# Casts of v for steps 4 to 7 on ScalarE, new engine orders, and other stores in two transfers, in a retention + SoLU kernel

## The chip, the core and the metric

The kernel runs on one core of a Trainium2 chip. A core has five engines, each with its own in-order list of instructions: TensorE (PE, matmuls and transposes, with its weight loads shown as PEld), VectorE (DVE), ScalarE (ACT), GpSimd (POOL) and SyncE (SP, which here does nothing but issue transfers). Engines wait for one another through semaphores. Data comes from HBM into SBUF by DMA; matmuls write PSUM. The metric is the device time of one execution in microseconds (us), the median over runs.

## The reference, cut to what matters

Inputs are q, k, v of shape 8 x 8 x 576 x 64 (batch, heads, positions, head dimension) and the weights of one feed-forward block, all float32.

```
scores = q @ k.T / 8                          # per batch and head, 576 x 576
ret    = scores * D                           # D[i,j] = gamma_h ** (i-j) for i >= j, else 0
x      = (ret @ v), heads side by side        # 4608 tokens x 512
h      = x @ w_in                             # 4608 x 1024
solu   = h * softmax(h)
ln     = (solu - mean) / sqrt(var + 1e-6) * g_ln
out    = ln @ w_out                           # 4608 x 512, float32
```

The kernel computes the first part as retention with a running state: positions are taken in windows of 256, and what lies before a window enters through a 64 x 64 state for each head instead of through scores.

## The kernel before

**Steps and tiles.** There are 18 windows: for each batch two of 256 positions (`wi` 0 and 1), and for every four batches one window that holds their last 64 positions (`wi` 2). A window is worked on in two *steps*, one for each half of the heads, so there are 36 steps `i` (two for each window), and it gives two *tiles* of 128 tokens, so there are 36 tiles `t`. Steps 4 and 5 are window 2 and give tiles 4 and 5.

**Operations of a step** (the name is that of the order lists, `x` stands for the number):

- `ldq`, `ldk`, `ldv` on SP (L363): one transfer of 256 KB each into one of five raw buffers (four of 64 KB in a `wi` 2 step).
- `sq`, `sk` (L379): scale by powers of gamma and cast to f16; `cv` (L387): cast v to f16. They run on POOL unless the table `ON` (L35) says otherwise.
- `K` on PE (L514): the new part of the state. `st` on DVE (L536) adds it, `sm` (L550) and `sc` (L554) on POOL decay it and cast it.
- `T` on PE (L403): transposes of q and k; `Te` or, joined with a transpose of a later stage, `TL` on ACT brings the result to SBUF (L441).
- `S` on PE (L489): scores; `mask` on DVE (L526) multiplies them by D. `I` on PE (L465): state part of the output; `V` (L504): the rest, added in the same PSUM tile `xy`; `xe` on ACT (L563) takes it to SBUF.

**Operations of a tile:** `M1` on PE (L571, eight 128 x 512 matmuls), `ex` on ACT (exponential, L582), `so` on DVE (L587), statistics as `bnA`, `bnB` on DVE or, for tiles 0 to 3, `va` on ACT, `fx` on ACT, `rs` on POOL; `L` on PE (transpose, L424), `Le` or `TL` on ACT, `M2` on PE (L643), `oe` on ACT (L654) and `out` on SP (L663), a store of 256 KB. There is one PSUM buffer for `h` (the result of `M1`, kept until `so`), one for `xy`, one for `s` (scores and, in turn, the result of most `M2`).

**Weights.** `lwi` and `lwo` load w_in and w_out in four transfers of 512 KB each; `wi` casts w_in, `wg` scales w_out by g, `WM` on PE (L706) forms column means and `wc` on DVE (L717) subtracts them. `M1_0` needs all `wi`, `M2_0` all `wc`.

**What sets the order.** `plan` (L123) lists all operations with their engine, dependences and buffers. Each engine issues its operations in the order of a key. `FIRST` (L42) and `LAST` (L78) spell the beginning and end out by hand; between them the key grows by 4.92 for each step. `order_ops` (L224) only models when each would start; from it the program takes the interleaving in which the instructions are emitted, and how many matmuls on zeros (L836) to put into expected gaps on PE before `M2_0`. They keep TensorE busy and change no result. On each engine the list is followed strictly: an operation that waits holds back all behind it on that engine.

Of the kernel before, what the change touches and what calls it, by code (L numbers as in the profile page):

```python
# [31 lines left out]
OFF = 6.0  # L32
NJ, NK, LAG, WE = 8, 8, 6, 0
VA = (0, 1, 2, 3)
ON = {'sq0': 'DVE', 'sq1': 'DVE', 'cv0': 'ACT', 'cv1': 'ACT', 'sk2': 'DVE', 'sk3': 'DVE', 'cv2': 'ACT', 'cv3': 'ACT'}  # L35
CAP = dict(
    rawq=5, rawk=5, rawv=5, q16=3, k16=4, v16=4, ev=8, s=1, ret=2, xy=1, gg=6, gt=2, s160=4, s161=9, h=1,
    e=2, solu=4, osb=3, tl=1, tlx=2, tlT=1, tlL=1, wst=5,
# [39 lines left out]
LAST = dict(  # L78
    PE=(
        "I34 L30 V34 S35 M1_32 I35 L31 V35 M2_28 M1_33 M2_29 M2_31 M1_34 L32 M2_30 L33 L34 M1_35 M2_32 M2_33 "  # L80
        "cs L35 M2_34 M2_35 M3"
    ),
    ACT=(
        "oe27 xe34 ex32 Le31 xe35 oe28 ex33 Le30 oe29 fx16 ex34 fx15 Le32 oe31 oe30 Le33 ex35 Le34 oe32 fx17 "
        "Le35 oe33 oe34 oe35 oz"
    ),
    DVE=(
        "so31 mask35 so32 bnA32 bnB32 bnA31 so33 bnB31 bnA33 so34 bnB33 bnA34 bnB34 so35 cnt bnA35 ci bnB35"
    ),
    POOL=(  # L90
        "rs15 rs16 rs17"
    ),
    SP=(
        "out27 out29 out28 out31 out30 out32 out33 out34 out35"
    ),
)

# [123 lines left out]
    return o.eng == "DVE" and o.name[:2] in ("sq", "sk", "cv", "wi", "wg")  # L221


def order_ops(ops):  # L224

    start, done, free = {}, {}, {"SP": 0.7, "PE": 5.7, "DVE": 4.5, "ACT": 4.0, "POOL": 3.5}
# [5 lines left out]
    quad, dma, lock, landed = False, 2.0, 0.0, []  # L232
# [16 lines left out]
    while len(start) < len(ops):  # L249
# [7 lines left out]
        x, o = best  # L257
# [41 lines left out]
def kernel(  # L299
# [489 lines left out]
    with tc.manual_schedule():  # L789
# [161 lines left out]
```

## Time and profile before

| | |
|---|---|
| median of 3 runs | 216.57 us (214.99 to 218.24) |
| profiled execution, its own time | 215.59 us |
| its span, first to last instruction | 213.9 us |
| PE busy | 201.8 us (94%) |
| POOL busy | 144.3 us (67%) |
| DVE busy | 166.7 us (78%) |
| ACT busy | 139.4 us (65%) |
| DMA | 42.67 MB, mean 200 GB/s |
| granted TensorE clock | 0.998 |

The profile is that of one execution. The span runs from its first instruction to its last; the execution's own time is 1.7 us longer. A timeline row gives the start, the length, the engine, the source line, the operation and what it writes and reads, and in brackets how long the engine was idle before it and what ended that. A row of windows gives, for a stretch, the busy time of each engine, the granted clock, the mean busy share of the DMA engines (it can pass 1) and the bytes moved a second. Since every engine follows its list, the rows can be laid beside the lists, so that each row has a name such as `cv5` or `M1_4`. PE's transfers of weights overlap its matmuls and matmuls overlap one another, so a busy PE is not one at its peak.

### The profile page before, as it was taken

The page shows a single profiled execution, that of the slowest core. Times are in us where ns is not written, and L with a number is a line of the kernel's source. Part 1 is how long each engine was busy: PE and PEld are TensorE (multiplying, and loading weights), DVE is VectorE, ACT ScalarE, POOL GpSimd, SP SyncE. Part 2 cuts the span into 40 slices and gives each one's busy share as a digit, 9 for nine tenths or more (in the row PEclk, how much of TensorE's full clock was granted, in tenths as well). Part 3 has the DMA queues.
Part 4 walks back from the last instruction along what each step waited for, and adds up shares of the span by engine and source line. Part 5 has one row for each costly group of instructions (what it writes and reads, how often), then busy time and mean ns, then how long its engine had stood idle before and what let it go on. Part 6 is the DMA issues. An engine that isn't in the chain of part 4 may idle for free. (4 is left out here: it accounts for less than half of the span.)

```text
span 213.9 us, 10164 instructions
## 1 busy us (share of the span) xinstructions
PE 201.8 (94%) x4408; PEld 114.5 (54%) x4408; DVE 166.7 (78%) x279; ACT 139.4 (65%) x231; POOL 144.3 (67%) x244
## 2 busy tenths in 40 slices
PE   7887999999999999999999999999999899999990
PEld 2453555565666565555555555665555555644450
DVE  6476678996888788978998889889989978565730
ACT  2355797866776667767667766777777666574750
POOL 8372869999997699747887979797979771000210
PEclk9999999999999999999999999999999999999999
DMA  6999999999676988698667778864355111104344
GB/s 166 321 373 320 340 315 280 297 266 266 169 215 186 320 268 241 165 291 262 199 213 214 209 219 232 226 209 146 104 150 186 52 54 52 52 3 98 90 105 110
DMA packets 64815, 42.67 MB, mean 200 GB/s; under 512 B 3320, under 2 KB 58624, under 8 KB 64768
## 3 DMA queue, kind: packets, MB, share of 16 engines
q1 hardware_dynamic: 64528, 41.82, 67.5%
q8 instruction: 35, 0.57, 1.1%
q10 hardware_dynamic: 240, 0.18, 0.3%
q14 instruction: 12, 0.10, 0.2%
HBM read 32.55 MB, written 9.44 MB: 196 GB/s over the span
## 5 line engine op out<-in xcount | busy, mean ns | idle before, releaser
L577 PE MATMUL h_ps<-w_in,xT 128*128 128x512 f16 x288 | 68.3, 380 | 0.7 <-DVE bs L606 0.7
L650 PE MATMUL o_ps<-w2c,ev 128*128 128x512 f16 (+1 forms) x296 | 67.6, 373 | 0.0
L585 ACT ACTIVATE e_sb<-h_ps 128x1024 f32<-128x1024 f32 x36 | 36.9, 1024 | 24.5 <-PE h_ps L577 24.5
L600 DVE TENSOR_TENSOR solu<-h_ps,e_sb 128x1024 f16<-128x1024 f32 x32 | 39.1, 1222 | 16.8 <-ACT e_sb L585 16.7
L530 DVE TENSOR_TENSOR ret<-s_ps,masks 128x1024 f16<-128x1024 f32 x36 | 44.0, 1223 | 6.1 <-PE s_ps L498 5.5
L650 PEld LDWEIGHTS <-ev 128*128 128x128 f16 x296 | 28.7, 98 | 32.7
L606 DVE BATCH_NORM_STATS2 bs<-solu 128x6 f32<-128x512 f16 x64 | 43.3, 685 | 0.8
L577 PEld LDWEIGHTS <-xT 128*128 128x128 f16 x288 | 25.6, 98 | 29.6 <-issue 1.0
L384 POOL TENSOR_TENSOR q<-rawq,small 128x512 f16<-128x512 f32 x34 | 35.4, 1042 | 6.3 <-DMA rawq<-in_q_dram 5.0
L659 ACT ACTIVATE o_sb<-o_ps,rs 128x512 f32<-128x512 f32 (+1 forms) x37 | 24.9, 675 | 20.6 <-PE o_ps L650 8.5
L384 POOL TENSOR_TENSOR k<-rawk,small 128x512 f16<-128x512 f32 x34 | 35.4, 1042 | 2.0 <-DMA rawk<-in_k_dram 1.6
L447 ACT COPY ev<-tl 128x1024 f32<-128x1024 f32 (+1 forms) x32 | 29.8, 931 | 5.3 <-PE tl L419 3.2
L566 ACT CAST xT<-xy 128x512 f16<-128x512 f32 x36 | 26.8, 744 | 6.0 <-PE xy L462 5.9
L561 POOL CAST sbd<-gg 64x256 f16<-64x256 f32 x64 | 25.7, 401 | 2.9
L552 POOL TENSOR_TENSOR gg<-gt,small 128x128 f32<-128x128 f32 x32 | 13.2, 414 | 16.2 <-DVE gt L547 15.5
L638 POOL TENSOR_TENSOR w<-mv,w 128x2 f32<-128x2 f32 x16 | 3.1, 194 | 29.3 <-ACT w L623 19.1
L389 POOL CAST v<-rawv 128x512 f16<-128x512 f32 x32 | 19.4, 608 | 3.5 <-DMA rawv<-in_v_dram 3.1
L836 PE MATMUL tl<-zeros 128*128 128x512 f16 x50 | 14.5, 422 | 1.3 <-DVE zeros L792 1.3
L498 PE MATMUL s_ps<-ev 64*64 64x128 f16 x576 | 14.9, 218 | 0.7 <-ACT o_sb L659 0.5
L462 PE MATMUL xy<-ret,v 64*64 64x128 f16 x576 | 14.7, 217 | 0.0
L436 PE MATMUL tl<-ident,solu 64*64 64x64 f16 x1024 | 14.3, 195 | 0.1
L462 PEld LDWEIGHTS <-sbd 128*128 128x128 f16 x128 | 9.2, 98 | 9.3 <-POOL sbd L561 1.5
(71 smaller groups left out, 213.8 us busy)
## 6 DMA issues: line engine op xcount, KB each, us to landing
rawk<-in_k_dram SPq DMA_DIRECT2D x32, 256.0 KB, 5.2
rawq<-in_q_dram SPq DMA_DIRECT2D x32, 256.0 KB, 5.1
rawv<-in_v_dram SPq DMA_DIRECT2D x32, 256.0 KB, 4.9
out_dram<-o_sb SPq DMA_DIRECT2D x26, 256.0 KB, 3.3
out_dram<-o_sb SPq DMA_DIRECT2D x19, 128.0 KB, 2.4
wst<-in_moe_w_in_dram SPq DMA_DIRECT2D x4, 512.0 KB, 6.9
wst<-in_moe_w_out_dram SPq DMA_DIRECT2D x4, 512.0 KB, 7.6
rawk<-in_k_dram SPq DMA_DIRECT2D x16, 64.0 KB, 3.2
```

The source lines that it names most:

```text
L384: eng.tensor_tensor(out=t.rearrange("p j h d -> p h j d"), in0=st[i]["r" + nm], in1=g, op=ALU.mult)
L447: nc.scalar.copy(out=t[:, lo:hi].rearrange("p x (r w) -> p r x w", r=2), in_=tls[n].rearrange("p r x w -> p (r x w)").bitcast(FP).rearrang ...
L462: nc.tensor.matmul(start=(c, e) not in begun, stop=False, skip_group_check=True, **kw)
L530: nc.vector.tensor_tensor(out=d["ret"].rearrange("p e h j q -> p (e h) (j q)"), in0=d["s"].rearrange("p e h j q -> p (e h) (j q)"), in1=ma ...
L561: nc.gpsimd.tensor_copy(out=t[ee[e], :, :, ee[e]], in_=st[i]["gg"][ee[e]])
L566: nc.scalar.copy(out=xT[:, 2 * w : 2 * w + 2, 2 * hf : 2 * hf + 2].rearrange("p c h (q j) -> p c h j q", j=2), in_=xys[i][:, :, 0:256].rea ...
L577: nc.tensor.matmul(out=h_ps[:, hh], lhsT=xT[:, t, dc], rhs=w_in16[:, dc, hh], start=(dc == 0), stop=(dc == 3),)
L585: nc.scalar.activation(out=d["e"], in_=d["h"], func=ACT.Exp, accum_out=se[:, t : t + 1])
L600: nc.vector.tensor_tensor(out=d["solu"], in0=d["h"], in1=d["e"], op=ALU.mult)
L606: nc.vector.bn_stats(out=d["bs"][:, half], in_=d["solu"][:, half * 512 : half * 512 + 512])
L650: nc.tensor.matmul(out=o, lhsT=d["ev"][:, d["lo"] + c], rhs=w2c16[:, c, mm], start=(c == 0), stop=(c == 7))
L659: nc.scalar.activation(out=d["osb"][:, mm], in_=d["o", half], func=ACT.Copy, scale=ws[t // 2]["rs"][:, t % 2 : t % 2 + 1])
```

## The change

Three things change, all in the same file.

- **Engine of four casts.** `ON` gets `cv4` to `cv7`: these casts of v go from POOL to ACT. Other casts stay.
- **Orders.** Nine of the ten hand-written lists are new; only the `LAST` of POOL is the same. The loads begin with q, k, v of steps 0 and 1, then all of w_in, then steps 2 and 3; before, step 2 came ahead of most of w_in. The loads of step 5's q and of `ldk5` come later than before, those of `ldk6` and `ldv6` earlier. `T8` moves ahead of `M1_4`, `S8` behind `K9`.
- **Stores.** Before, tiles from 28 on went out in two transfers of 64 rows; now tiles 22 to 27 do, and 28 to 33 go in one. Tiles of a `wi` 2 window (16, 17, 34, 35) always take two. A new function `parts` tells the model in `order_ops` into how many transfers each load and store falls, and the model counts each of them.

The computation is the same in both. The diff, cut to the lists up to about `M1_5` and the code:

```diff
-ON = {'sq0': 'DVE', 'sq1': 'DVE', 'cv0': 'ACT', 'cv1': 'ACT', 'sk2': 'DVE', 'sk3': 'DVE', 'cv2': 'ACT', 'cv3': 'ACT'}
+ON = {'sq0': 'DVE', 'sq1': 'DVE', 'cv0': 'ACT', 'cv1': 'ACT', 'sk2': 'DVE', 'sk3': 'DVE', 'cv2': 'ACT', 'cv3': 'ACT', 'cv4': 'ACT', 'cv5': 'ACT', 'cv6': 'ACT', 'cv7': 'ACT'}
...
 FIRST = dict(
     PE=(
-        "K0 T0 T1 S0 K1 I0 S1 V0 T2 I1 S2 V1 K2 M1_0 K3 T3 I2 S3 V2 M1_1 K4 L0 T4 I3 V3 S4 L1 M1_2 T5 K5 WM "
-        "S5 K6 M1_3 I4 V4 K7 T6 I5 S6 V5 T7 M1_4 I6 S7 V6 T8 K8 L2 T9 M2_0 L3 I7 S8 V7 K9 M1_5 M2_1 I8 L4 V8 "
+        "T0 S0 K0 K1 T1 I0 S1 V0 I1 V1 M1_0 K2 T2 T3 K3 S2 M1_1 I2 S3 V2 L0 I3 V3 T4 L1 K4 S4 M1_2 K6 WM K5 "
+        "M1_3 T5 K7 T6 I4 S5 V4 T7 I5 S6 V5 T8 M1_4 I6 S7 V6 K8 T9 L2 M2_0 I7 L3 V7 K9 S8 M1_5 M2_1 I8 L4 V8 "
...
     ACT=(
-        "cv1 cv0 Te0 Te1 cv2 wi3a wi2a xe0 Te2 wi1a xe1 wi0a cv3 ex0 Te3 xe2 wg4 wg6 ex1 Te4 Le0 xe3 wg0 Le1 "
-        "wg2 ex2 Te5 va1 fx0 va2 ex3 xe4 va0 Te6 xe5 fx1 Te7 va3 ex4 Te8 Le2 xe6 oe0 xe7 Le3 ex5 Te9 oe1 xe8 "
+        "cv0 cv1 Te0 Te1 wi2a wi1a xe0 wi0a wi3a xe1 cv2 ex0 Te2 cv3 Te3 wg4 wg0 ex1 xe2 cv4 Le0 xe3 Te4 Le1 "
+        "wg6 wg2 cv6 ex2 cv5 va1 cv7 ex3 Te5 va2 Te6 xe4 fx1 fx0 Te7 xe5 va0 Te8 ex4 xe6 Le2 va3 oe0 xe7 Le3 "
...
     DVE=(
-        "sq0 sq1 st0 st1 sk2 mask0 wi3b mask1 wi1b wi2b wi0b sk3 st2 mask2 st3 so0 wg7 mask3 st4 wg5 so1 "
-        "mask4 wg3 wg1 st5 so2 wc2 st6 wc4 mask5 wc1 wc0 st7 so3 mask6 wc3 wc7 wc6 wc5 mask7 fin0 so4 st8 "
+        "sq0 sq1 st0 mask0 st1 wi1b mask1 wi2b wi3b wi0b sk2 sk3 st2 so0 st3 wg5 mask2 mask3 so1 st4 wg7 wg1 "
+        "wg3 mask4 st6 so2 st5 wc4 wc0 wc7 wc1 st7 so3 mask5 wc5 wc2 wc6 mask6 wc3 mask7 fin0 st8 so4 mask8 "
...
     POOL=(
-        "sk1 sk0 sm0 sc0 sm1 sq2 sc1 sq3 sm2 sk4 sc2 sm3 sc3 cv4 sq4 sm4 sq5 sk5 cv5 sk6 sm5 cv6 sc5 sc4 cv7 "
-        "sk7 sq6 sm6 sq7 sk8 cv8 sc6 sq8 sk9 sq9 sm7 cv9 sc7 rs0 sq10 sm8 sq11 cv10 sk10 sc8 sm9 rs1 sk12 "
+        "sk0 sk1 sm0 sc0 sm1 sc1 sq2 sq3 sm2 sc2 sm3 sc3 sk4 sq4 sk6 sm4 sc4 sk5 sm6 sk7 sm5 sq5 sc5 sq6 sq7 "
+        "sk8 sq8 sk9 sc6 cv8 sq9 sm7 sc7 rs0 sq10 cv9 sq11 sm8 cv11 sk10 sc8 cv10 sk11 rs1 sm9 sc9 sq12 sm10 "
...
     SP=(
-        "ldk1 ldk0 ldq0 ldv1 ldv0 ldq1 lwi3 ldk2 ldv2 ldq2 lwi2 lwi1 lwi0 ldk3 ldq3 ldv3 ldk4 lwo4 lwo6 ldv4 "
-        "ldq4 lwo0 ldq5 ldk5 lwo2 ldv5 ldk6 ldv6 ldk7 ldk8 ldv7 ldk9 ldq6 ldq7 ldv9 ldv8 ldq8 ldq9 ldv11 "
+        "ldq0 ldk0 ldv0 ldv1 ldq1 ldk1 lwi1 lwi2 lwi0 lwi3 ldk2 ldv2 ldq2 ldk3 ldq3 ldv3 lwo4 lwo0 ldk4 ldq4 "
+        "ldv4 lwo6 ldk6 lwo2 ldv6 ldk5 ldv5 ldk7 ldq5 ldv7 ldq6 ldk8 ldq7 ldq9 ldq8 ldk9 ldv8 ldv11 ldq11 "
+        "ldk13 ldq10 ldv9 ldq12 ldk10 ldv12 ldv14 ldk11 ldq14 ldk14 ldv10 out0 ldv13 ldk12 ldq13 out2 ldq15 "
+        "out1 ldk15 ldq17 ldk17 ldq16 out3 ldv16 ldk16 ldv15 ldv17 ldv20 ldk18 ldq18 ldv21 out4 ldq19 out5 "
...
 LAST = dict(
     ACT=(
-        "oe27 xe34 ex32 Le31 xe35 oe28 ex33 Le30 oe29 fx16 ex34 fx15 Le32 oe31 oe30 Le33 ex35 Le34 oe32 fx17 "
-        "Le35 oe33 oe34 oe35 oz"
+        "oe27 xe34 ex32 Le30 Le31 oe28 xe35 ex33 fx15 oe29 ex34 Le32 oe30 Le33 oe31 fx16 ex35 oe32 Le34 oe33 "
+        "Le35 fx17 oe34 oe35 oz"
...
     SP=(
-        "out27 out29 out28 out31 out30 out32 out33 out34 out35"
+        "out29 out28 out27 out30 out31 out32 out33 out34 out35"
...
+def parts(name):
+
+    if name[:2] == "lw":
+        return 1
+    n = int(name[3:])
+    if WINS[n // 2][1] == 2:
+        return 2 if name[:3] == "out" else 4
+    return 2 if name[:3] == "out" and 22 <= n < 28 else 1
...
         if o.eng == "SP":
-            if len(landed) >= 7:
-                free["SP"] = end = max(end, landed[-7])
-            dma = max(end + 1.0, dma) + o.moved + (0.9 if len(landed) == 2 else 0.0)
-            landed.append(dma + 0.8)
-            done[o.name] = dma + 0.8
+            end, np = x, parts(o.name)
+            for _ in range(np):
+                end = max([end + o.dur / np] + landed[-7:-6])
+                dma = max(end + 1.0, dma) + o.moved / np + (0.9 if len(landed) == 2 else 0.0)
+                landed.append(dma + 0.8)
+            free["SP"], done[o.name] = end, dma + 0.8
...
         if wi < 2:
             r0 = b * S + 256 * wi + P * c
-            n = P if t < 28 else 64
+            n = 64 if 22 <= t < 28 else P
             for r in range(0, P, n):
                 nc.sync.dma_start(out=out[r0 + r : r0 + r + n, :], in_=tk[t]["osb"][r : r + n])
```

## The prediction

> **What bounds the kernel now.** I read the table of busy time first, then the slices, then windows of five to twenty us, then the timelines of each engine up to 50 us, laid beside the order lists. The chain that ended last is of no help: it holds one piece, the last eviction. Busy time and slices of the page:
>
> ```profile
> PE 201.8 (94%) x4408; PEld 114.5 (54%) x4408; DVE 166.7 (78%) x279; ACT 139.4 (65%) x231; POOL 144.3 (67%) x244
> ...
> PE   7887999999999999999999999999999899999990
> ...
> POOL 8372869999997699747887979797979771000210
> ...
> DMA  6999999999676988698667778864355111104344
> ```
>
> PE leads, and its gaps are all in the first eight slices (5.35 us each) and the last. Early DMA is at 9 while PE is at 7 or 8. Part of PE's early time is no work either:
>
> ```profile
> L836 PE MATMUL tl<-zeros 128*128 128x512 f16 x50 | 14.5, 422 | 1.3 <-DVE zeros L792 1.3
> ```
>
> So PE's real work is about 201.8 - 14.5 - 1.1 (three more on another tile) = 186 us, and what can be won lies where PE fills or idles. The windows say when that ends (columns: window, its length, busy time of PE, PEld, DVE, ACT, POOL, clock, DMA share, GB/s):
>
> ```profile
> 10.00:15.00 5.00, 4.40 (x88) 2.46 (x86) 3.64 (x9) 2.58 (x5) 3.40 (x6) 1.00 1.10 364
> 20.00:25.00 5.00, 3.65 (x70) 2.20 (x69) 3.84 (x8) 2.74 (x5) 4.54 (x8) 1.00 1.07 354
> 35.00:40.00 5.00, 4.82 (x59) 2.42 (x57) 4.78 (x10) 4.04 (x8) 4.85 (x8) 1.00 1.10 298
> 40.00:50.00 10.00, 9.39 (x195) 6.48 (x195) 8.55 (x15) 6.06 (x13) 9.72 (x16) 1.00 1.04 275
> 50.00:60.00 10.00, 10.00 (x261) 5.85 (x260) 8.75 (x17) 7.57 (x12) 9.72 (x16) 1.00 0.74 199
> ```
>
> To about 42 us the transfers run flat out (share over 1); from 50 us PE is full: idle after that is 0.9 us up to its last matmul at 208.45. PE's timeline gives the tiles' `M1`:
>
> ```profile
> 18.43 1.89 PE L577 MATMUL h_ps<-w_in,xT 128*128 128x512 f16 x8
> 24.30 1.90 PE L577 MATMUL h_ps<-w_in,xT 128*128 128x512 f16 x8
> 29.43 1.89 PE L577 MATMUL h_ps<-w_in,xT 128*128 128x512 f16 x8
> 34.79 1.90 PE L577 MATMUL h_ps<-w_in,xT 128*128 128x512 f16 x8
> 41.65 1.89 PE L577 MATMUL h_ps<-w_in,xT 128*128 128x512 f16 x8
> ```
>
> These are `M1_0` to `M1_4`; `M1_5` is at 49.84, and later tiles follow every 4.9 to 5.0. After `M1_4` both lists ask the same of PE, one operation for another. So the rule of the sum: **the end moves by as much as the moment from which PE is full**, that is by `M1_4`, plus real work done ahead of it, plus waits gone between it and `M1_5`.
>
> The Trainium skill (Perfetto Trace Analysis, section Identifying the Most-Contended Engine) speaks against such a reading: matmul occupancy is not to be taken as nearness to the roofline. The trace agrees as far as a row goes: `M1` is eight matmuls of 380 ns in 1.89 us, so they start 0.216 apart and the rows overlap. By that rule alone an order could gain after 50 us too; the starts, though, follow one another there without a hole.
>
> **The change, part by part.** When data lands. Counted in transfers of 256 KB (a weight is two), the consumers that waited for DMA show landings: the 6th at 9.34 (`sq1`), the 13th by 14.73 (`wi2a`), the 17th at 17.46 (`wi0b`), the 20th at 20.68 (`cv3`), the 33rd at 30.57 (`wg3`), the 34th at 31.57 (`cv5`), the 35th at 32.45 (`sk6`): 0.78 us each from the 20th on. I keep this curve and put the new list on it: w_in complete (14th) 15.3, k2 v2 q2 16.0 to 17.4 (before: about 11.7 to 13.4), v3 20.7, v4 26, `lwo2` (32nd) 29.9, v6 30.6, k5 31.4, v5 32.3, k7 33.1, q5 33.9, v7 34.7, q6 35.5, q7 37.0.
>
> Now the chain, with durations of before: f16 casts on ACT 0.62, `sq`/`sk` on POOL 1.04 (on DVE 0.69 alone, 1.11 beside POOL), `cv` on POOL 0.61, `sm` 0.40, `sc` 0.83, `ex` 1.11, `so` 1.22, `mask` 1.22, `xe` 0.74, `Te` 0.58, `wc` 0.70, a hop between engines 0.05.
>
> - `M1_0`: `wi3a` 15.3 to 15.9, `xe1` behind it on ACT to 16.65, so 16.7 (18.43).
> - `M1_1`: `sk3` on DVE from 19.0, `st2`, `so0` to 21.5; `sq3` on POOL to 21, then `T3 K3 S2`: 22.0 (24.30).
> - `M1_2`: `cv4` 26.2, `xe3` to 28.1, `K4`, `Te4`, `S4`: 29.0 (29.43).
> - `M1_3`: ACT casts `cv6` at 30.6, `ex2` 31.2 to 32.3, `so2` to 33.6: 33.7 (34.79).
> - `M1_4`: POOL has no pause from k7 on: `sk7` 33.1, `sm5`, `sq5` 34.8 to 35.85, `sc5`, `sq6` to 37.75, `sq7` 38.8, `sk8`, `sq8` 40.85. So `T6` 37.8 with `I4 S5 V4` queued behind it to 39.0. On ACT `cv7` 34.7, `ex3` 35.6, `Te5`, `va2`, `Te6`, `xe4` to 39.8; on DVE four `wc` to 37.1, `st7`, `so3` 39.0, `mask5` to 40.25; hence `S6` 40.3, `V5` to 40.9, `xe5` to 41.7 and `M1_4` at 41.75 (41.65).
>
> The lead of 1 to 2 us of the first tiles is thus used up where step 5's q, seven transfers later than before, meets POOL and PE's order. Term one: **+0.1**. The four casts free 4 x 0.61 = 2.4 us of POOL, which is at 97% from 40 to 60 us, and `sq8` ends at 40.85 instead of 43.57; but PE is full by then, so it buys only that `T8` fits ahead of `M1_4`: **-0.5** (T8 to K8, 44.27 to 44.82, leaves the full stage). On ACT they cost 4 x 0.62, with 40% of ACT free; behind them wait `Le0` (`cv4`), `ex2` (`cv6`), `va1` (`cv5`), `ex3` (`cv7`). `cv7` would end 0.3 before `ex3` can start; that slack is the cover, beyond it each us costs one.
>
> From `M1_4` to `M1_5`: before, `S8` waited to 49.15 for `oe0` (`M2_0` and the scores share a PSUM tile) while PE had ended `I7` at 48.65. Behind `L3 V7 K9` that wait is covered: **-0.5**. Walking the new list with `sk9` 41.9, `sc6` 42.75, `sq9` 44.4, `mask7` to 45.5, `M2_0` 45.6, `oe0` to 48.25, I get `M1_5` at 48.95 against 49.84, which is the three terms' sum.
>
> Middle: SP stands at `out2` (`oe2` ended at 59.26 before) with the loads of steps 15 to 17 behind it, but steps 12 to 14 are issued ahead of it, better than before, where `cv14` waited on DMA to 72.35. `T15` is due at 79. I take 0; bounds -0.9 (all idle after 50 us) and +1 (two more waits of the 0.4 us kind). Zero-fills: PE stands up to 1.46 us behind the longest burst after 9 us (six); new bursts are unknown, -1.5 to +1.5, taken as 0, since the rows show them ending before the operation they precede was ready.
>
> End: the halves of tiles 22 to 27 are six more issues on SP of under 0.6 us at 164 to 185 us, with nothing queued behind. Whole stores land later (3.3 against 2.4 us), and `out27` now waits behind `out29`; `oe30` needs its buffer and `M2_32` needs `oe30`: about 199.2, wanted at 200.76. `xe35` slips behind `oe28` to 190.8, `M2_31` wants it at 192.56. The last chain, `M3` to `oz` (208.54 to 209.02) to `out35`, is the same. 0, at worst +0.9.
>
> **Sum:** +0.1 - 0.5 - 0.5 = -0.9: 215.59 becomes 214.7 by the profiled execution. The median of the runs stands 0.98 above that execution, so the time I give is 216.57 - 0.9 = **215.7**. Landings off by 1 us shift `M1_4` by about 1, so alone this case spans 213.5 to 218.
>
> **Rivals.**
>
> *Loads speed up (faster).* The best window moved 364 GB/s, the 41 transfers up to q7 took 35 us at 307. At 364 they end 5.5 us sooner. `M1` cannot follow at less than 4.4 (as `M1_32` to `M1_33`, bound by `ex` and `so`), and POOL's unbroken row moves along: some 4 us, **211.7**. Against: DMA is at 9 in nearly every early slice already, and the mix up to there is the same bytes. The Trainium skill (HBM Reference, section Specifications (TRN2)) has one core alone at about 425 GB/s; the best row here is 364, so no row shows it.
>
> *ScalarE held by a cast (slower).* `cv6` and `cv7` stand ahead of `ex2` and `ex3`. Issue to landing was 2.9 to 9.3 us, so a v may come 3 us after its turn on the curve. If v6 or v7 lands more than 0.3 us late, `ex`, `so`, the next `M1` and `S6` all follow, us for us; one of them 3 us late gives **218.7**, both give 221.7. For it: 6.4 us of ACT's idle time before were waits for v already. Against: POOL's `cv5` waited 1.1 us for the same data, not more.
>
> *The freed POOL is worth nothing and neither is the rest*: 216.6, inside the forecast's range.
>
> **How the numbers follow.** Forecast and nothing-gained 0.68, faster rival 0.14, slower rival 0.18. Runs of before differ by 1.5%, so 2% is about what a measurement can tell from no change: 212.2 and 220.9. Faster beyond it 0.13 (the faster rival nearly whole), slower 0.14 (two casts late, or an unseen wait in the middle), within 0.73. The range 212.4 to 220.0 leaves some 0.1 on each side.
>
> **What would show it.** `M1_0` near 16.7, `M1_1` 22, `M1_3` 33.7, `M1_4` 41 to 42.5, `T8` ahead of it; `S8` without a wait; `M1_5` 48.5 to 49.5; PE full behind it, last matmul near 207.6; ACT waiting under 0.5 us for `cv7`. Wrong if `M1_4` is off by over 2 us, or if PE idles over 1.5 us between 55 and 180 us.

## The result, and the profile after

| | before | after |
|---|---|---|
| median of 20 runs each | 215.94 us (214.69 to 219.28) | 218.62 us (216.25 to 220.22) |
| profiled execution, its own time | 215.59 us | 219.43 us |
| its span | 213.9 us | 217.7 us |
| PE idle from 50 to 60 / from 60 to 100 us | 0.0 / 0.25 us | 0.48 / 3.93 us |
| granted TensorE clock | 0.998 | 0.988 |

The ratio of the times, after to before, is 1.009 with a 95% interval of 1.0065 to 1.0115. The ratio leaves out runs that are more than 1.5% above the fastest of their kernel, here and in the ratios below, while the medians hold all runs. The changed kernel is about 0.9% slower: 0.009 x 215.94 is 1.9 us. Within 2% was the likeliest class and 218.62 lies in the range, but 0.9 us of gain was forecast, and the sign is wrong.

The page of the kernel after, busy time and slices (a slice is now 5.44 us):

```profile
PE 202.2 (93%) x4400; PEld 113.5 (52%) x4400; DVE 166.3 (76%) x279; ACT 141.3 (65%) x235; POOL 141.6 (65%) x240
...
PE   7797969999999967998999999999999999999992
...
POOL 7435658998994846863879797978979794001110
PEclk9999999999999996999999999999999999999998
DMA  6999999999175479299876866777345322203233
```

The totals differ by little: POOL has 2.7 us less and ACT 1.9 more, as four casts of 0.6 us should give. What is new stands in the middle. DMA, at 9 from the second slice on, falls to 1 in the eleventh (54 to 60 us). Four slices later PE falls to 6, and in the next the granted clock does. The windows of the kernel after (columns as in the prediction):

```profile
10.00:15.00 5.00, 4.58 (x88) 2.64 (x88) 4.05 (x9) 3.29 (x6) 2.76 (x7) 1.00 1.07 374
20.00:25.00 5.00, 4.41 (x94) 2.99 (x95) 3.68 (x7) 3.90 (x7) 3.93 (x9) 1.00 1.12 333
35.00:40.00 5.00, 4.55 (x82) 2.65 (x80) 4.68 (x9) 4.16 (x8) 4.81 (x7) 1.00 1.13 298
40.00:50.00 10.00, 9.56 (x197) 6.32 (x195) 8.43 (x13) 8.67 (x18) 9.69 (x16) 1.00 1.11 289
50.00:60.00 10.00, 9.52 (x259) 5.56 (x257) 8.66 (x17) 6.34 (x11) 8.88 (x15) 1.00 0.56 170
60.00:100.00 40.00, 36.07 (x832) 19.95 (x833) 29.40 (x46) 23.83 (x39) 27.54 (x47) 0.96 0.68 206
```

Up to 50 us all is as before or better. From 50 to 60 us the transfers are at 0.56 (before 0.74), and from 60 to 100 us PE stands for 3.93 of 40 us. PE's timeline of the kernel after shows both halves of the story (start, length, operation, and in brackets the idle time before it and what ended that):

```profile
15.33 1.92 PE L587 MATMUL h_ps<-w_in,xT 128*128 128x512 f16 x8
21.57 1.90 PE L587 MATMUL h_ps<-w_in,xT 128*128 128x512 f16 x8
28.26 1.90 PE L587 MATMUL h_ps<-w_in,xT 128*128 128x512 f16 x8
34.23 1.90 PE L587 MATMUL h_ps<-w_in,xT 128*128 128x512 f16 x8
41.88 1.91 PE L587 MATMUL h_ps<-w_in,xT 128*128 128x512 f16 x8
48.99 1.25 PE L587 MATMUL h_ps<-w_in,xT 128*128 128x512 f16 x5
...
74.89 1.90 PE L587 MATMUL h_ps<-w_in,xT 128*128 128x512 f16 x8
...
80.37 0.28 PE L472 MATMUL xy<-ev,sbd 128*128 128x128 f16 x2 [1.85 <-POOL sbd L571]
81.49 0.32 PE L429 MATMUL tl<-ident,k 64*64 64x64 f16 x16 [0.33 <-POOL k L394]
83.13 0.64 PE L508 MATMUL s_ps<-ev 64*64 64x128 f16 x16 [1.10 <-ACT o_sb L669]
83.91 3.02 PE L587 MATMUL h_ps<-w_in,xT 128*128 128x512 f16 x8
```

The rows of L587 are `M1_0` to `M1_5`, `M1_10` and `M1_11`. `M1_5` begins at 48.99 against 49.84, 0.85 us early. `M1_10` is still 0.45 early (75.34 before). `M1_11` is 3.63 late (80.28 before), and from there the delay stays: `M1_12` +4.97, `M1_35` +5.06. Between `M1_10` and `M1_11` PE waits three times, for `sbd` of step 13 (`sc13`), for k of step 15 (`sk15`) and for `oe6`. Then `M1_11` takes 3.02 us instead of 1.90, since the clock is down.

The books close but for 0.7 us. From `M1_5` to `M1_35` the kernel loses 5.06 + 0.85 = 5.91 us. PE idles 0.48 + 3.93 = 4.41 us there, and 0.91 before (0.25 up to 100 us, and 0.66 just ahead of `M1_29`), so 3.50 more; the clock was at half for 3.4 us, which costs up to 1.7: together 5.2. Where the other 0.7 us went stays open. At the end 1.2 us come back in this execution, because less time lies behind the last eviction (3.64 against 4.86 us). So 5.06 - 1.2 = 3.86 against the 3.84 us between the two executions.

**What PE waited for.** The chain goes back to SP. Its timeline in the kernel after, from the last load ahead of the gap to `ldv15` (a row gives when SP began to issue and how long that took; L680 is a store):

```profile
51.05 0.66 SPq L379 DMA_DIRECT2D rawq<-in_q_dram  x1
58.85 0.36 SPq L680 DMA_DIRECT2D out_dram<-o_sb  x1
...
61.78 2.09 SPq L384 DMA_DIRECT2D rawq<-in_q_dram  x4
63.96 2.91 SPq L384 DMA_DIRECT2D rawk<-in_k_dram  x4
66.98 1.81 SPq L384 DMA_DIRECT2D rawq<-in_q_dram  x4
...
69.31 3.00 SPq L384 DMA_DIRECT2D rawv<-in_v_dram  x4
72.41 1.80 SPq L384 DMA_DIRECT2D rawk<-in_k_dram  x4
74.25 0.44 SPq L379 DMA_DIRECT2D rawv<-in_v_dram  x1
```

The second row is `out2`. The list of waits of SP from 48 to 64 us (who waited, for what: us in total, times, longest) puts a number on it:

```profile
SPq L680 <- ACT o_sb L669: 7.0, 1, 7.0
```

SP stands for 7.0 us until `oe2` ends at 58.83, and no load leaves. Behind that come `ldq15`, `out1` and `ldk15`, then the loads of the `wi` 2 steps, four transfers of 64 KB each, which take SP 1.8 to 3.0 us (2.09 + 2.91 + 1.81 + 3.00 + 1.80 = 11.6 us for five of them). So `ldv15` goes at 74.25. POOL's timeline shows what hangs on it:

```profile
70.58 2.04 POOL L394 TENSOR_TENSOR q<-rawq,small 128x512 f16<-128x512 f32 x2 [2.85 <-DMA rawq<-in_q_dram]
...
78.91 0.61 POOL L399 CAST v<-rawv 128x512 f16<-128x512 f32 x1 [3.46 <-DMA rawv<-in_v_dram]
79.46 0.85 POOL L571 CAST sbd<-gg 64x256 f16<-64x256 f32 x2
80.39 1.04 POOL L394 TENSOR_TENSOR k<-rawk,small 128x512 f16<-128x512 f32 x1
```

`sq16` waits 2.85 us for its q and `cv15` 3.46 us for its v. Behind `cv15` stand, in POOL's order, `sc13`, `sk15` and `rs3`. They are what PE waited for in this execution, `rs3` by way of `oe6` on ACT, in whose PSUM tile `S14` wants to write.

### The profile page after: what moved, and what is told of

Same layout as the page of the kernel before. It is cut to its first block, busy times and chain, and to the rows that moved or that the text cites. A ratio compares the mean times of both kernels' runs of the same rounds, so it can differ in the third digit from the quotient of the medians.

```text
span 217.7 us, 10155 instructions
## 1 busy us (share of the span) xinstructions
PE 202.2 (93%) x4400; PEld 113.5 (52%) x4400; DVE 166.3 (76%) x279; ACT 141.3 (65%) x235; POOL 141.6 (65%) x240
## 5 line engine op out<-in xcount | busy, mean ns | idle before, releaser
L587 PE MATMUL h_ps<-w_in,xT 128*128 128x512 f16 x288 | 69.5, 385 | 0.0
L587 PEld LDWEIGHTS <-xT 128*128 128x128 f16 x288 | 25.6, 99 | 29.8 <-issue 1.5
L399 POOL CAST v<-rawv 128x512 f16<-128x512 f32 x28 | 17.0, 609 | 4.5 <-DMA rawv<-in_v_dram 4.3
L472 PE MATMUL xy<-ev,sbd 128*128 128x128 f16 (+1 forms) x128 | 12.2, 213 | 2.2 <-POOL sbd L571 1.8
```

Of the source, the lines that this page charges most:

```text
L472: nc.tensor.matmul(start=(c, e) not in begun, stop=False, skip_group_check=True, **kw)
L587: nc.tensor.matmul(out=h_ps[:, hh], lhsT=xT[:, t, dc], rhs=w_in16[:, dc, hh], start=(dc == 0), stop=(dc == 3),)
```

## The experiments

These theories go through the expectations. **A**: the place of `out2` in SP's list makes the loss. In reading **A1** its wait alone does it; in **A2** the loads must also be put in the order of need, since the five raw buffers would hold `ldk15` back until `sk13`. **B**: the casts on ScalarE, or the start, do it. **C**: POOL's order, with `sq16` and `cv15` far ahead, turns late loads into a stall. **S0**: the choice of stores in two transfers is worth nothing. The lines with a minus in a diff are those of the changed kernel, unless said otherwise. "Idle" is PE's idle time from 60 to 100 us in the profile. The runs come in three groups, and each ratio is against the kernel before in the same group, on the same chip; its medians there are 216.09 us (e1 to e4), 216.41 (e5 to e8) and 217.58 (e9, e10, b1 and b2).

### e1: the loads of steps 15 to 17 by need

```diff
-        "ldk13 ldq10 ldv9 ldq12 ldk10 ldv12 ldv14 ldk11 ldq14 ldk14 ldv10 out0 ldv13 ldk12 ldq13 out2 ldq15 "
-        "out1 ldk15 ldq17 ldk17 ldq16 out3 ldv16 ldk16 ldv15 ldv17 ldv20 ldk18 ldq18 ldv21 out4 ldq19 out5 "
+        "ldk13 ldq10 ldv9 ldq12 ldk10 ldv12 ldv14 ldk11 ldq14 ldk14 ldv10 out0 ldv13 ldk12 ldq13 ldq15 out1 "
+        "ldq17 ldv16 ldq16 out2 ldk15 ldk17 out3 ldv15 ldk16 ldv17 ldv20 ldk18 ldq18 ldv21 out4 ldq19 out5 "
```

> The changed kernel, with eleven entries of SP's list in another order: out2, ldk15 and ldk17 go behind ldq17, ldv16 and ldq16, and ldv15 ahead of ldk16. Theory A (SP's line): in the changed kernel SP stood from 51.7 to 58.85 us at out2 and to 61.4 at ldk15 with the loads of steps 16, 17 and of v15 behind them; they landed at 70.4 (q16) and 78.8 (v15), POOL waited 2.85 and 3.46 us for them and PE 3.6 us, from M1_10 to M1_11. With the loads ahead, q16 lands by 64, v15 by 70, M1_11 follows M1_10 by 5.0 to 5.4 us instead of 9.0, PE idles under 0.8 us from 60 to 100 us, and the time is 3.5 to 5 us below the changed kernel's: ratio to the kernel before 0.988 to 0.997. Theory B (the casts on ScalarE cost the time): no change, ratio 1.009. Theory C (POOL's order, sq16 and cv15 too far ahead): waits for data go, so the gain is the same as by A; only the run with cv15 moved tells A and C apart.

Measured: 214.72 us, ratio 0.9947 (0.9915 to 0.9978). `M1_11` at 79.80, idle 0.78 us. The loss is gone and the gain is there, so A holds and B is not needed. A1 and A2 are not told apart by it.

### e2: only `out2` moves

```diff
-        "ldk13 ldq10 ldv9 ldq12 ldk10 ldv12 ldv14 ldk11 ldq14 ldk14 ldv10 out0 ldv13 ldk12 ldq13 out2 ldq15 "
-        "out1 ldk15 ldq17 ldk17 ldq16 out3 ldv16 ldk16 ldv15 ldv17 ldv20 ldk18 ldq18 ldv21 out4 ldq19 out5 "
+        "ldk13 ldq10 ldv9 ldq12 ldk10 ldv12 ldv14 ldk11 ldq14 ldk14 ldv10 out0 ldv13 ldk12 ldq13 ldq15 out1 "
+        "ldk15 ldq17 ldk17 ldq16 out2 out3 ldv16 ldk16 ldv15 ldv17 ldv20 ldk18 ldq18 ldv21 out4 ldq19 out5 "
```

> The changed kernel with out2 alone moved, behind ldq16. If out2 alone holds SP's line (A1), all of the loss comes back: ratio 0.988 to 0.997. If ldk15 holds it as well (A2), since its raw buffer is free only when sk13 ends on POOL at 61.0, SP stands there instead, q17, k17 and q16 are issued within 0.5 us of the changed kernel's times (61.8, 64.0, 67.0), and the time stays: ratio 1.005 to 1.011. I hold A2. Theory B: 1.009.

Measured: 214.86 us, ratio 0.9936 (0.9907 to 0.9966), as good as e1. One name moved by six places in one list is worth 1.009 - 0.9936 = 1.5% of the time, 3.3 us (from two groups of runs; by the ratios of e5 and e8 below, of one group, it is 1.0% or 2.2 us). SP's timeline of e2:

```profile
53.84 0.36 SPq L680 DMA_DIRECT2D out_dram<-o_sb  x1
54.30 0.38 SPq L379 DMA_DIRECT2D rawk<-in_k_dram  x1
...
70.04 1.47 SPq L379 DMA_DIRECT2D rawv<-in_v_dram  x1
```

The first row is `out1`, the second `ldk15`: it goes at 54.30, long before `sk13` (60.4 us on POOL), so A2's reason, a full set of raw buffers, was wrong. `ldv15` goes at 70.04 instead of 74.25. POOL's timeline of e2:

```profile
74.17 0.61 POOL L399 CAST v<-rawv 128x512 f16<-128x512 f32 x1 [0.51 <-DMA rawv<-in_v_dram]
```

`cv15` waits 0.51 us instead of 3.46. The windows of e2:

```profile
50.00:60.00 10.00, 9.66 (x259) 5.56 (x257) 8.67 (x17) 6.37 (x12) 8.89 (x15) 1.00 1.04 286
60.00:100.00 40.00, 39.50 (x992) 22.73 (x984) 33.49 (x53) 27.71 (x45) 30.04 (x52) 1.00 0.69 207
```

PE is idle for 0.50 us from 60 to 100, and the DMA engines move 286 GB/s from 50 to 60 us where the changed kernel moved 170.

### e3: only POOL's order moves

```diff
-        "sq13 sk14 sk13 sc10 sk12 cv12 sm11 rs2 cv13 sq14 sc11 sm12 sq16 sq15 sc12 cv14 sm13 sk17 cv15 sc13 "
-        "sk15 rs3 sk16 sm14 sc14 sm15 sk18 sc15 sq17 cv17 rs4 cv16 rs5 sq18 cv18 sq19 sk19"
+        "sq13 sk14 sk13 sc10 sk12 cv12 sm11 rs2 cv13 sq14 sc11 sm12 sq16 sq15 sc12 cv14 sm13 sk17 sc13 sk15 "
+        "rs3 cv15 sk16 sm14 sc14 sm15 sk18 sc15 sq17 cv17 rs4 cv16 rs5 sq18 cv18 sq19 sk19"
```

> The changed kernel with cv15 alone moved on POOL, from ahead of sc13 to behind rs3. v15 still lands near 78.8, but sc13, sk15 and rs3 no longer wait behind it, so I13, T15 and (through oe6) S14 are ready by 79; K15 then waits for cv15 at 79.4. By theory C (POOL's order turns a late load into a stall) M1_11 starts at 79.8 to 80.5 instead of 83.9, and 3 to 4.5 us come back: ratio 0.99 to 0.998. By theory A in its strict form (the late load itself is the stall) K15 and what follows wait all the same and under 1.5 us come back: ratio 1.003 to 1.009. Theory B: 1.009.

Measured: 215.92 us, ratio 0.9983 (0.995 to 1.0017), idle 2.39 us. v of step 15 is still late (`cv15` could start at 76.9), but `M1_11` comes at 80.34, on time; `M1_12` is at 86.96, 1.8 us late against 85.15 before. By the ratios some two thirds of the loss, 1.009 - 0.9983 of 1.009 - 0.9936, come back without touching SP; e4 below, in the same group and with the same stall, has 1.0098. So the late load seems to do its harm mostly through what is queued behind `cv15` on POOL, not through its own consumer. The profile alone shows less: in it v15 landed at 76.9 us, where it came at 78.8 in the changed kernel, so that the old order, too, would have lost less there.

### e4: the four casts back on POOL

```diff
-ON = {'sq0': 'DVE', 'sq1': 'DVE', 'cv0': 'ACT', 'cv1': 'ACT', 'sk2': 'DVE', 'sk3': 'DVE', 'cv2': 'ACT', 'cv3': 'ACT', 'cv4': 'ACT', 'cv5': 'ACT', 'cv6': 'ACT', 'cv7': 'ACT'}
+ON = {'sq0': 'DVE', 'sq1': 'DVE', 'cv0': 'ACT', 'cv1': 'ACT', 'sk2': 'DVE', 'sk3': 'DVE', 'cv2': 'ACT', 'cv3': 'ACT'}
...
-        "sk0 sk1 sm0 sc0 sm1 sc1 sq2 sq3 sm2 sc2 sm3 sc3 sk4 sq4 sk6 sm4 sc4 sk5 sm6 sk7 sm5 sq5 sc5 sq6 sq7 "
...
+        "sk0 sk1 sm0 sc0 sm1 sc1 sq2 sq3 sm2 sc2 sm3 sc3 sk4 cv4 sq4 sk6 sm4 sc4 cv6 sk5 cv5 sm6 sk7 cv7 sm5 "
+        "sq5 sc5 sq6 sq7 sk8 sq8 sk9 sc6 cv8 sq9 sm7 sc7 rs0 sq10 cv9 sq11 sm8 cv11 sk10 sc8 cv10 sk11 rs1 sm9 "
...
```

`cv4` to `cv7` leave ACT's list and stand in POOL's where their data is due.

> The changed kernel with cv4 to cv7 back on POOL, behind sk4, sk5, sc4 and sk7, and the other lists kept. Theory B (the casts in ScalarE's line are the loss): the time falls to that of the kernel before or below, ratio 0.99 to 1.0. Theory A: the casts were no loss; POOL gets 2.4 us more work between 24 and 36 us, M1_4 comes 0.5 to 1.5 us later than 41.9, sk13 and with it ldk15 and the late loads by as much, the stall at M1_11 stays: 0 to 2 us above the changed kernel, ratio 1.009 to 1.018.

Measured: 218.55 us, ratio 1.0098 (1.0058 to 1.0138). The loss stays, so the casts are not its cause; nor is the start, which e2 keeps. So B falls. PE's timeline of e4, `M1_4` and `M1_5`:

```profile
42.68 1.91 PE L587 MATMUL h_ps<-w_in,xT 128*128 128x512 f16 x8
49.99 1.90 PE L587 MATMUL h_ps<-w_in,xT 128*128 128x512 f16 x8
```

In this execution `M1_4` comes 0.8 and `M1_5` 1.0 us later than in the changed kernel. `M1_5` of after, e2, e5 and b1, which have the start in common, lies between 48.28 and 49.46, and of e4 at 49.99, where the kernel before has 49.84: in this one execution the early start shows no gain without the casts on ACT. Yet the times of e4 and of the changed kernel are alike. With the stall of SP in place, the start's gain doesn't reach the end.

### e5: e2 with the old choice of stores

The lines with a minus are e2's.

```diff
-    return 2 if name[:3] == "out" and 22 <= n < 28 else 1
+    return 2 if name[:3] == "out" and n >= 28 else 1
...
-            n = 64 if 22 <= t < 28 else P
+            n = P if t < 28 else 64
```

> The kernel with out2 moved (e2), and the stores in two transfers those of tiles 28 to 35 again, as in the kernel before. Stores land 2.4 us after issue as halves and 3.4 whole, but out35 alone ends the run, and it has two halves in both. Theory S0 (the choice of halves costs nothing): ratio 0.990 to 0.997, as e2 had, 0.9936. Theory S1 (six issues fewer at the end let out35 land earlier, since it landed 2.6 us after its issue in the changed kernel's profile and 3.7 in that of before): 0.8 to 1.2 us slower than e2, ratio 0.997 to 1.0. I hold S0, because one run with whole stores also had 3.6 us there.

Measured: 214.09 us, ratio 0.9911 (0.9867 to 0.9955); e2 had 0.9936, and the intervals overlap; b1 and b2 below, which differ in the stores alone, lie the other way round. No effect of the stores can be seen, as S0 says; one of some 0.5% would not be.

### e6: the same mistake put into the kernel before

The lines with a minus are those of the kernel before; `out0`, `out1` and `out2` go ahead of `ldk16`.

```diff
-        "ldq4 lwo0 ldq5 ldk5 lwo2 ldv5 ldk6 ldv6 ldk7 ldk8 ldv7 ldk9 ldq6 ldq7 ldv9 ldv8 ldq8 ldq9 ldv11 "
-        "ldv12 ldv13 ldq11 ldq10 ldk11 ldk10 ldv10 ldq12 ldq13 ldk12 ldk17 ldq15 ldv15 ldk16 out1 ldv17 ldk13 "
-        "out0 ldk15 ldv16 ldk14 ldq16 ldq14 ldv19 out2 ldv14 ldq18 out3 ldk20 ldk18 ldq19 out5 ldq21 ldk22 "
-        "out4 ldq17 out6 ldv21 ldv18 ldq20 ldk19 ldv20 out7 ldk21 ldq22 ldv22 out8 ldq23"
+        "ldq4 lwo0 ldq5 ldk5 lwo2 ldv5 ldk6 ldv6 ldk7 ldk8 ldv7 ldk9 ldq6 ldq7 ldv9 ldv8 ldq8 ldq9 ldv11 ldv12 "
+        "ldv13 ldq11 ldq10 ldk11 ldk10 ldv10 ldq12 ldq13 ldk12 ldk17 ldq15 ldv15 out0 out1 out2 ldk16 ldv17 "
+        "ldk13 ldk15 ldv16 ldk14 ldq16 ldq14 ldv19 ldv14 ldq18 out3 ldk20 ldk18 ldq19 out5 ldq21 ldk22 out4 "
+        "ldq17 out6 ldv21 ldv18 ldq20 ldk19 ldv20 out7 ldk21 ldq22 ldv22 out8 ldq23"
```

> The kernel before, with out0, out1, out2 moved up in SP's list to behind ldv15, and nothing else. It puts the suspected wait into the kernel that hadn't it: SP stands from 51.5 us until oe2 ends at 59.3, with the loads ldk16, ldv17, ldk13, ldk15 and so on behind it. ldk13 was issued at 58.1 and would be at about 65; sk13 on POOL, 62.24 before, waits to 69 or 70, and st/sm of later steps behind it. Theory A (a store in SP's line ahead of loads costs the time): PE idles 3 to 7 us between 60 and 90 us, ratio 1.012 to 1.03. Theory B (the casts or the other orders): no effect, ratio 0.998 to 1.002.

Measured: 221.01 us, ratio 1.0202 (1.0151 to 1.0254), idle 5.17 us. SP's waits from 48 to 92 us and PE's timeline of e6:

```profile
SPq L670 <- ACT o_sb L659: 5.6, 2, 4.6
```

```profile
71.59 0.29 PE L462 MATMUL xy<-ev,sbd 128*128 128x128 f16 x2 [2.75 <-POOL sbd L561]
73.02 1.90 PE L577 MATMUL h_ps<-w_in,xT 128*128 128x512 f16 x8
79.78 0.32 PE L419 MATMUL tl<-ident,q 64*64 64x64 f16 x16 [2.42 <-POOL q L384]
81.27 2.96 PE L577 MATMUL h_ps<-w_in,xT 128*128 128x512 f16 x8
```

Old order, old casts, old stores, and the same picture: SP held by stores, PE waiting for POOL, a slow `M1` behind it. The mechanism needs nothing else of the change. It hits another tile (`M1_9` at 73.02 instead of 69.93), because other loads stand behind.

### e7: `out2` half way

```diff
-        "ldk13 ldq10 ldv9 ldq12 ldk10 ldv12 ldv14 ldk11 ldq14 ldk14 ldv10 out0 ldv13 ldk12 ldq13 out2 ldq15 "
-        "out1 ldk15 ldq17 ldk17 ldq16 out3 ldv16 ldk16 ldv15 ldv17 ldv20 ldk18 ldq18 ldv21 out4 ldq19 out5 "
+        "ldk13 ldq10 ldv9 ldq12 ldk10 ldv12 ldv14 ldk11 ldq14 ldk14 ldv10 out0 ldv13 ldk12 ldq13 ldq15 out1 "
+        "out2 ldk15 ldq17 ldk17 ldq16 out3 ldv16 ldk16 ldv15 ldv17 ldv20 ldk18 ldq18 ldv21 out4 ldq19 out5 "
```

> The changed kernel with out2 moved two places only, behind ldq15 and out1. SP still stands at it to 58.85, but goes on with ldk15 at 59.2 instead of 61.4. All later loads come 2.1 us earlier: q16 at 68.3, v15 at 76.7. POOL's wait for q16 falls from 2.85 to about 0.8, that for v15 stays near 3.4, so I13 is in time, T15 and S14 are 1 to 1.5 us late and M1_11 starts at 81.3 to 82.0 (83.9 in the changed kernel, 80.06 with out2 behind ldq16). Theory A: half of the loss comes back, ratio 0.999 to 1.005. If the wait at out2 had a threshold instead (all or nothing): 0.994 or 1.009.

Measured: 215.73 us, ratio 0.995 (0.9918 to 0.9983), under the 0.999 to 1.005 that was expected. In its group it lies between e5's 0.9911 and e8's 1.0014, and its interval overlaps both, so half can't be told from most. The profiled execution was one of the slowest of the kernel (217.72 us) and can't stand for the median run. In it `oe2` came late (PE had waited 1.42 us for `cv10`), SP went on with `ldk15` at 60.55 instead of 59.2, `ldv15` left at 74.47, no earlier than in the changed kernel, and `M1_11` is at 84.04, the full stall. How the loss grows with `out2`'s place stays open.

### e8: the changed kernel again

No edit: is the loss the same in another group of runs?

> The changed kernel itself, once more, on the same chip as these. Ratio 1.006 to 1.012. Its profile again has SP standing at out2 for 6.5 to 7.5 us, POOL waiting 2 to 4 us each for q16 and v15, and 3 to 4 us between M1_10 and M1_11 beyond the usual 5.0. Open: whether the granted clock falls to 0.5 for 3.4 us after that idle time, as it did once (M1_11 took 3.02 us instead of 1.90) and did not with the casts back, where PE idled 3.1 us in the same stretch.

Measured: 217.50 us (215.13 to 221.53), ratio 1.0014 (0.9972 to 1.0056). The interval lies under the 1.006 that was expected. The loss against the kernel before was thus about 0.9% in one group and, by the ratio, too small to tell in the other (by the medians of all runs, 217.50 to 216.41, it is 0.5%); single runs spread over 3% where those of e2 spread over 1.3%. What holds in both is that the mended list is faster: e5 has 0.9911 in the same group, and the two intervals lie apart. This execution's profile shows the stall without a fall of the clock: idle 2.18 us, `M1_11` at 82.47. SP stands at `out2` for 7.1 us as expected, but POOL then waits 4.38 us for q16 and only 0.43 for v15, where 2 to 4 us each were expected. PE's longest wait is therefore for `sc12`, behind `sq16`: 1.58 us ahead of `M1_10` (at 76.78), and 0.60 us for `oe6` follow ahead of `M1_11`. e4's profile has the same form (4.75 and 0.37 us on POOL, 1.95 us on PE). So of the two late loads now one and now the other reaches PE.

### e9: `ldv15` three places earlier

```diff
-        "out1 ldk15 ldq17 ldk17 ldq16 out3 ldv16 ldk16 ldv15 ldv17 ldv20 ldk18 ldq18 ldv21 out4 ldq19 out5 "
+        "out1 ldk15 ldq17 ldk17 ldq16 out3 ldv15 ldv16 ldk16 ldv17 ldv20 ldk18 ldq18 ldv21 out4 ldq19 out5 "
```

> The changed kernel with out2 left where it is and ldv15 alone moved, from behind ldv16 and ldk16 (eight transfers of 64 KB) to right behind out3. SP still stands at out2 for some 7 us, q16 still comes at about 70.4 and POOL still waits 2 to 3 us for it, but v15 is issued at 69.3 instead of 74.3 and lands by 73, before POOL comes to cv15 at 75.5. Theory A' (out2's wait and the eight small issues make up v15's delay together, and v15 alone reaches PE): I13, T15 and S14 are in time, M1_11 follows M1_10 by 5.0 to 5.6 us, 2.5 to 4 us come back, ratio 0.992 to 0.999. If q16's delay reaches PE by itself: under 1.5 us come back.

Measured: 217.07 us, ratio 0.9974 (0.9938 to 1.0009). The profiled execution, slower than the median at 218.32 us, has `M1_11` at 80.71 as expected, but the stall returns one tile later, `M1_12` at 88.40. The waits from 80 to 92 us name the reason:

```profile
ACT o_sb L669 <- DMA out_dram<-o_sb: 3.3, 1, 3.3
```

`oe7` stands 3.3 us for a store buffer, which `out4` frees. `out4` is queued on SP behind the late loads and leaves at 80.91 (75.72 in e2); it lands some 6 us later, in a stretch (81 to 87 us) with the DMA engines at 1.00. PE then waits 2.04 us for `oe7`. So on a late SP a store that stands behind loads can become the next wait.

### e10: a second store in the way

```diff
-        "ldk13 ldq10 ldv9 ldq12 ldk10 ldv12 ldv14 ldk11 ldq14 ldk14 ldv10 out0 ldv13 ldk12 ldq13 out2 ldq15 "
-        "out1 ldk15 ldq17 ldk17 ldq16 out3 ldv16 ldk16 ldv15 ldv17 ldv20 ldk18 ldq18 ldv21 out4 ldq19 out5 "
+        "ldk13 ldq10 ldv9 ldq12 ldk10 ldv12 ldv14 ldk11 ldq14 ldk14 ldv10 out0 ldv13 ldk12 ldq13 out2 out3 "
+        "ldq15 out1 ldk15 ldq17 ldk17 ldq16 ldv16 ldk16 ldv15 ldv17 ldv20 ldk18 ldq18 ldv21 out4 ldq19 out5 "
```

> The changed kernel with out3 moved up to right behind out2: the suspected wait is lengthened. SP stands until oe3 ends at 64.0 instead of oe2 at 58.8, so every load from ldq15 to ldv17 comes some 4.5 to 5 us later still; q16 lands at 75, sc12 behind it misses I12 (due at 73.5), v15 lands at 83. Theory A: 4 to 6 us on top of the changed kernel, ratio 1.022 to 1.036. If the loads behind out2 had slack and the loss came from elsewhere: as the changed kernel, 1.001 to 1.009.

Measured: 223.46 us (four runs, 220.43 to 228.48), ratio 1.0284 (1.0191 to 1.0377), as expected: a longer wait on SP costs more. Of its waits from 64 to 80 us:

```profile
POOL q L394 <- DMA rawq<-in_q_dram: 7.3, 1, 7.3
...
PE xy L472 <- POOL sbd L571: 4.5, 1, 4.5
```

`sq16` now waits 7.3 us (2.85 in the changed kernel), and PE 4.5 us behind it.

### b1 and b2: the mends together

b1 takes e2's and e3's edits, and `ldv10` ahead of `ldq14 ldk14`, since PE of the changed kernel and of e2 waited 0.36 and 0.34 us for `cv10`. b2 has the old choice of stores in addition.

```diff
-        "sq13 sk14 sk13 sc10 sk12 cv12 sm11 rs2 cv13 sq14 sc11 sm12 sq16 sq15 sc12 cv14 sm13 sk17 cv15 sc13 "
-        "sk15 rs3 sk16 sm14 sc14 sm15 sk18 sc15 sq17 cv17 rs4 cv16 rs5 sq18 cv18 sq19 sk19"
+        "sq13 sk14 sk13 sc10 sk12 cv12 sm11 rs2 cv13 sq14 sc11 sm12 sq16 sq15 sc12 cv14 sm13 sk17 sc13 sk15 "
+        "rs3 cv15 sk16 sm14 sc14 sm15 sk18 sc15 sq17 cv17 rs4 cv16 rs5 sq18 cv18 sq19 sk19"
...
-        "ldk13 ldq10 ldv9 ldq12 ldk10 ldv12 ldv14 ldk11 ldq14 ldk14 ldv10 out0 ldv13 ldk12 ldq13 out2 ldq15 "
-        "out1 ldk15 ldq17 ldk17 ldq16 out3 ldv16 ldk16 ldv15 ldv17 ldv20 ldk18 ldq18 ldv21 out4 ldq19 out5 "
+        "ldk13 ldq10 ldv9 ldq12 ldk10 ldv12 ldv14 ldk11 ldv10 ldq14 ldk14 out0 ldv13 ldk12 ldq13 ldq15 out1 "
+        "ldk15 ldq17 ldk17 ldq16 out2 out3 ldv16 ldk16 ldv15 ldv17 ldv20 ldk18 ldq18 ldv21 out4 ldq19 out5 "
```

> A version meant to beat both: the changed kernel with out2 behind ldq16, ldv10 ahead of ldq14 and ldk14 (K10 waited 0.3 us for cv10 and that for v10), and cv15 behind rs3 on POOL. M1_5 at 48.3 to 49.3, PE idle from 50 to 100 us under 0.7 us in sum: ratio 0.988 to 0.994.

> The same as b1, with the stores in two transfers those of tiles 28 to 35, as in the kernel before. By S0 (stores cost nothing either way) within 0.003 of b1; if the halves of the last tiles help, 0.003 to 0.006 lower.

Measured: b1 213.86 us, ratio 0.9821 (0.9772 to 0.987); b2 214.42 us, 0.9859 (0.9814 to 0.9904). Both beat the kernel before and, by their ratios, the changed one. b1's interval lies below the expected 0.988 to 0.994; the kernel before was slower in this group than in the others. b2 is 0.0038 above b1 where at most 0.003 was expected, with intervals that overlap. By medians b1 is 1.0 us below e2 and 0.2 below e5; whether it is better than these isn't shown. The windows of b1, PE idle for 0.33 and 0.34 us:

```profile
50.00:60.00 10.00, 9.67 (x259) 5.70 (x258) 8.96 (x17) 6.56 (x12) 8.94 (x15) 1.00 0.98 280
60.00:100.00 40.00, 39.66 (x1026) 23.09 (x1024) 33.36 (x53) 27.54 (x45) 30.19 (x52) 1.00 0.72 218
```

## Why the prediction was right or wrong

- **The rule of the sum** (the end moves with the moment from which PE is full) needs PE to stay full, and so it failed here: PE was full from 49 us as forecast, and then not. Where the stall is taken out, it holds: e2's ratio of 0.9936 is 1.4 us of gain where the three terms gave 0.9.
- **The start chain: right.** `M1_4` at 41.88 for 41.75 forecast (41.65 before): the +0.1 measured +0.2. `M1_5` at 48.99 for 48.95. The steps between were less exact: `M1_0` came 1.4 us earlier than forecast, `M1_1` 0.4, `M1_2` 0.7 and `M1_3` 0.5 later. The errors of the early ones did not carry, since step 5's q and POOL's row behind it set `M1_4`, as the walk said.
- **T8 ahead and S8's wait covered: right together.** From `M1_4` to `M1_5` it is 7.11 us instead of 8.19, 1.08 less for the 1.0 that the two terms gave.
- **The casts on ACT: right.** v7 landed at 35.1 for 34.7 forecast, and `cv7` began at 35.18, and no wait on PE came of it; the slower rival (a cast holds ScalarE) did not come. That its 218.7 us lies beside the measured 218.62 is chance. What the move is worth may have been under-rated: POOL's freed time was credited with `T8` alone, 0.5 us, while `M1_5` in e4's one profile is 0.5 to 1.7 us later than in those with the casts on ACT.
- **The faster rival: no.** The best window moved 374 GB/s against 364 (a slice of the page of before already had 373), and v7's landing kept to the old curve.
- **Middle: wrong. This is the step that failed:** "SP stands at `out2` ... with the loads of steps 15 to 17 behind it ... `T15` is due at 79. I take 0; bounds -0.9 ... and +1". The stand was named and then priced at nothing. The move of `out2` alone measured 3.3 us (e2 against the changed kernel), or 2.2 us within one group (e5 against e8): two to three times the upper bound. Three things were missing. The length of the stand was not worked out, though rows of before held it: SP of before had issued 52 entries of its list by 51.5 us, the new list has 54 ahead of `out2`, and `oe2` ended at 59.26, so an estimate of 7 us (7.0 measured). What comes after the stand was not counted: the loads behind it are mostly in four parts, and they cost 1.8 to 3.0 us each (the five such rows of before between 48 and 67 us have 1.8 to 3.4). And the due time was taken from `T15` on PE, where it had to be taken from POOL's list: `sc12` stood behind `sq16`, and `sc13` of an earlier step behind `cv15`; in the profile of after PE wanted `sc13` at 78.5, not at 79, with `sk15` and `rs3` after it. By e3's ratio this order, not the load alone, makes most of the loss.
- **After the start, one operation for another: right.** From `M1_15` to `M1_29` it is 69.31 us (105.95 to 175.26) against 69.84 (100.38 to 170.22, with a wait of 0.66 us ahead of `M1_29`), so where nothing waits the new orders are worth 0.5 us at most. By the page of the Trainium skill that the prediction weighed (Perfetto Trace Analysis, section Identifying the Most-Contended Engine), more could have come there; these rows don't show it.
- **Zero-fills and end: 0, right within what can be seen.** e5 finds no difference by the stores. The matmuls on zeros fell from 53 to 45; no run shows what they alone are worth. The time behind the last eviction was 1.2 us less in the profile of after, but it comes out at one or the other with both choices (below), so it is no gain of the change.
- **The sign to look for was right**: "if PE idles over 1.5 us between 55 and 180 us" names what happened, 3.93 us from 60 to 100.

Open: what decides which of the late loads reaches PE and whether the clock falls, so why the loss differs from run to run (e8), and what it is as a function of `out2`'s place (e7).

## What to carry to other kernels

In an engine's list that issues transfers, every entry that waits for a result is a gate for all loads behind it: for each such entry, work out when its result comes, when the engine would reach it, and add the issue time of what is queued behind before you ask when a load lands. Then take the due time of that load from the list of the engine that consumes it, with everything that stands behind the consumer there, not from the last user. A store that goes late costs only its buffer, but put it too far back and that becomes the wait (e9).

## What the runs showed of the hardware

**The clock falls after short gaps, in some executions.** In the profile of after, the granted clock was 0.5 for 3.4 us from 82.8 us on. The window that holds most of the fall, with the clock at 0.72 in the mean and PE busy throughout:

```profile
84.00:88.00 4.00, 4.00 (x14) 1.59 (x15) 2.30 (x5) 1.76 (x3) 2.05 (x5) 0.72 0.95 313
```

From 78.5 us on PE had waited 1.85 and 0.33 us and stood in the gap of 1.10 us when it came, never 3.4 us in one piece. The same fall of 3.4 us came in e6 (from 80.0 us), e9 (87.9) and e10 (77.6, there in a gap of 4.51 us in one piece), but not in e4, e7 and e8: e4 idled for 3.11 us from 60 to 100 and kept its clock, e9 for 2.16 and lost it. Of the 20 runs of the changed kernel, the 10 with a mean clock under 0.995 have a median of 219.14 us, the other 10 of 217.59: 1.55 us, near the 1.7 that half a clock for 3.4 us costs. In e8 the five runs with mean clocks of 0.982 to 0.990 took 218.76 to 221.53 us, the seven with 0.995 to 1.000 took 215.13 to 217.83. (The mean also counts a fall behind the last matmul, which costs PE nothing: 0.78 from 213.6 us on in the profile of after.) That this explains the spread is argued from these rows; no experiment here set the clock. The Trainium skill (TensorE: Matmul & The Clock Gate, section What's actually happening) says that the gate has two states, half and full, watches windows of about 3.4 us that run on freely, and goes down after one idle window. The trace agrees with the half clock and with the 3.4 us, and with its coming in some executions only; but in after, e6 and e9 gaps of at most 2.75 us with work in between were enough, where that section's words ask for an idle window.

**The issue of a load in four parts of 64 KB** took SP 1.8 to 3.6 us in these profiles, a load of 256 KB in one part mostly 0.4 to 0.6, at times up to 3.4. Behind the stand it seems to be the issue, not the bytes, that spaced the loads: from 60 to 78 us of the kernel after, the DMA share was only 0.57.

**The last store** (the half that SP issues) landed 2.3 to 3.7 us after its issue, with both choices of stores: 3.7 in before and in e4, 2.6 in after and in e5. One profile's tail says nothing on a change of the end.
